# Attention and ReGLU on one core: one written list for the first three tiles, and all lists drawn up anew

## The chip, the cores and the metric

The kernel runs on one core of a Trainium2 chip. Its time is device microseconds (us) of one execution, as the median of several runs. Besides the runs there is one execution that the hardware profiler took; a profile shows that one.

## The reference

```python
# q, k, v: (8 batches, 8 heads, 576, 64); block 64; scale 1/8
scores = scale * q @ k^T, masked to (row // 64 >= column // 64)
attn   = exp(scores - max) / (sum + 1e-09) @ v
x      = attn as (4608 tokens, 512)
out    = (max(x @ w_gate, 0) * (x @ w_val)) @ w_out    # d_ff 1536
```

Blockwise causal attention gives the rows of x, and a gated feed-forward network (ReGLU) follows.

## The kernel before

The feed-forward part is cut into nine tiles of 512 tokens. Tile j, from 0 to 7, is the first 512 tokens of batch j; tile 8 is the eight tails of 64 tokens. Attention runs in visits, one for two heads of one batch: visit r = 4 * batch + pair of heads. A visit computes scores (`s` or `A`, L611), exponentials on ScalarE (`e` or `E`, L616 and L623), zeroes in the corners that the mask excludes (`c` or `C`, L1526 on VectorE, L1529 on POOL), the products with v (`a`, `b` or `V`, L759), a normalisation on VectorE, and a transpose of the result into xT, from visit 4 on by a DMA of SP's queue (`x` or `T`, L842). Attention for a batch is done while the feed-forward part of an earlier tile runs.

Everything is under a manual schedule: each engine executes its instructions in the order in which the program issues them, and waits on semaphores where data or buffers are not ready. So the written order is the order on every queue, SP's and POOL's DMA queues among them.

Tiles 0 to 2 come from a generator, `ffn_gen` (L1156). `ffn(n)` advances it by n matmuls of 512 columns, and the other work of this time, the "acts" (loads, casts, visits of batches 0 to 3, sums of weights), has place numbers in a dictionary `AT`, so that an act is issued when the generator has done that many matmuls. A negative number orders what stands ahead of the first of them. The acts that the text names:

- `j0` to `j4` are filler matmuls on zeros (L1517) that keep TensorE running at the start; `M0` is the first transposing of q and k on TensorE (L420), `p00` the first scores (L561), `x0` to `x3` are the transposes of batch 0's visits into xT.
- `s8` to `s11`, `a8` to `a11`, `b8` to `b11` and `x8` to `x11` are the visits of batch 2: scores, the products with v of the two heads, and the transpose. `s12` opens the visits of batch 3 and is the first to read the transposed tail qTt.
- `d3` and `d4` transpose q and k of batches 3 and 4 (`dma_transposes`: qTm and kTm at L499, qTt at L504, kTt at L506), all on SP's queue; `l4` and `lv4` load batch 4 on POOL's DMA queue (L489).
- `U..` is one sum of weight blocks, `up_sum` (L950); `W..` and `D..` are further weight sums and differences (L901, L904, L915). `on(name)` (L918) gives an operation to POOL if its name is in `ON_POOL`, else to VectorE.

From tile 3 on, a product of matrices is done by seven products of half-size blocks in place of eight, so that sums of blocks on VectorE and POOL replace matmuls. `program(j)` (L1307) returns `do(t)`, which carries out one item of a written list: `ORDER_3_6` for tiles 3 to 6, `ORDER_7` and `ORDER_8`. In these lists `pnw` is work on pair n of hidden blocks: a digit w is half of one of the products (256 columns, L1348), and a letter an operation on the results: `a`, `b` copies on ScalarE (L1371, L1374), `s` a sum (L1377), `m`, `y`, `z` additions out of PSUM on VectorE (L1382, L1393, L1396), `r`, `l` on ScalarE, `H` and `L` the two halves of the hidden product (L1401, and L1415 on VectorE). `s` with four digits forms block sums of the hidden values for the down-projection (L992), `M1` to `M7` are its seven products (L1033), `oa` to `od` and the other `o` items combine them (L1080), and `S` stores. `X` are sums of x (L1154), `g`, `v`, `r`, `h` the pairs that are done with plain products (L1322, L1445).

Buffers rotate by strings too: `SLOTS` gives for each tag (the PSUM banks sc and ffnp, the SBUF tiles ob and gate_sb) which buffer the next tile takes, and `PAIR_BANK` and `AV_BANK` say in which banks the results of a pair or of a visit's products with v lie. A list and these strings are drawn up together.

The corners of a visit in tiles 3 to 6 are issued here:

```python
corners(
    4 * up + i,
    zero_pool if f"{i}C" in ON_POOL else zero_dve,
    (((0, 512),), ((896, 128),))[c],
)
```

`ON_POOL` has no entry that ends in C, so all these memsets run on VectorE.

Of the kernel before, what the change touches and what calls it, by code (L numbers as in the profile page):

```python
# [17 lines left out]
def kernel(  # L18
# [12 lines left out]
    B, H, S, D = q.shape  # L31
# [14 lines left out]
            "010101010101010010101010101010101010101010101010101010101001110010100110"  # L46
            "100111001010011010011100101001101001110010100110100110100101"
        ),
        "ffnp": (
            "021021021020210210210210210210120210120202010101210120201201120120210211"  # L50
            "201021102101020120120120121201202101202101202101210210201102220201101202"
            "001201202112000202112102022102102011022202011012020012012021120002021121"
            "0202210210122001201200121012012"
        ),
        "ob": (
            "043210432104310420312142324014203124304232410421302431423240142031243042"
            "324104210324103140231403"
        ),
        "gate_sb": (
            "021021021021021021021021021021021021021021011201201002102101120120100210"  # L60
            "21021021"
        ),
    }
    ORDER_3_6 = """
        A0 E0t X1 X3 X4 X6 Y4 g0 X7 E0u E0s C01 E0f g0 K g0*2 r0 k g1*2 v0*2 C00 l0 l1
        l2 v0 p15 v0 h0 p15 p1a g1*2 V00 U02 N00 r1 P V01 N01 p12*2 p1b p1s p13 l3 w0
        p13 p1r p11 v1*2 p11 l4 l5 p1m p14 p16*2 p1y d0 p14 p1l v1 U01 U06 U42 l6 l7 l8
        d1 d2 A1 E1u v1 h1 p17*2 p32 E1t E1s E1f p25*2 p32 g8 p1z p1L C11 p22*2 g8*2
        p35*2 C10 s0101 p1H s0112 p2a p23*2 p2b p24 p21 g8 p21 p24 p3b p2r p26 s0012 l9
        l10 d3 w1 p3a p3s s0001 p26 p2s p2m p2y p2H p33*2 p31*2 p3m p2l p27*2 p2z p3r  # L70
        p36*2 p3y r8 p34*2 p3l V11 N11 A2 E2t E2u E2f p2L p37*2 p3z U41 w2 w3 p52*2
        s1101 p55*2 s0212 p3L p5b v8*2 V10 N10 p51 v8*2 h8 p5a p53*2 p51 p54 p5s p5m E2s
        C21 g9*2 p54 s1201 p5r p56 g9 p56 g9 p5l p57 r9 p57 v9*4 p5y p5z C20 h9 M3*2 A3
        E3t p5L s2001 E3s p3H U45 s1012 s2101 s1112 s1001 E3u p5H s2112 U05 E3f U07
        s2012 V21 N21 C31 M4 M3*2 M4 M3*2 U46 U47 w4 w5 C30 V20 N20 M1*3 M4*3 T1 T0 oa
        M5 M1*2 M4 ob V31 M5 V30 M5 N31 M5*2 T2 N30 T3 M1 M5 M2*4 oy M2*2 S0 oz s0201
        s2212 s1212 S1 s2201 M6*2 om M7 M6*3 oc od M7 M6 M7*4 o6 S2 o7
    """
    ORDER_7 = """
        p15 p05 X1 p05 p0a p02*2 p0b p12*2 p1b p01 X3 X4 p03 p0s p03 p0r p15 p1a p04*2  # L80
        p0l p01 p1s X6 p06*2 p13*2 p1r p25*2 X7 p07*2 p0m p0y p0H Y1 p0z p0L p11 p22*2
        p11 P p2a p2b p2s p23*2 p2r p16 p14*2 p1l p16 p1m p1y p24 p26 p21*2 p26 s0101
        p24 p2l p1H p35*2 p3a p2m p2y p32*2 p27*2 p45 p3b p3s p45 p4a s0001 p2H p2z
        p17*2 p1z p33 p34 p33 p55 p42*2 p3r p34 p31*2 p2L p4b p4s p1L p3l p36*2 p55 p5a
        p3m p3y p3H s1101 p43*2 p4r p44 p37*2 p3z p3L s0112 p52 p41 p46 p52 p5b p41 p4m
        p53*2 p5r p5s p51 p44 p4l p51 p46 p4y p54 p47 p56 p54 p4H p5m p56 p5y p5l M4 p47
        p4z p57*2 p5z M3 M4 M3 M1 p5H M4*4 p4L p5L s1012 s1112 M3 s2112 s2101 M3*3 oa
        s0012 s1001 M1*5 M5 s2001 M5 s2012 M5*4 oy S0 ob M2*5 s0212 s0201 M6 s1201 s2212
        M2 M7 s1212 M6 s2201 oz S1 M6 M7 M6*3 om oc od o6 Y3 M7*4 o7 S2
    """  # L90
    ORDER_8 = """
        X6 p12*2 p1b p15*2 p1a p1s X7 p02*2 p0b p05*2 p14 p11*2 p13*2 p0a p0s p1m p01
        p03 p14 p01 p0m p03 p1r p16*2 p1y p1H p1l p17*2 p1z p0r p06*2 p04*2 P p0y p22*2
        p1L p0l p0H p2b s0112 p25*2 p32*2 p35 p07 p35 p2a p2s p07 p0z p0L p23*2 p3a p24
        p21*2 p2m p24 p2r p26*2 p3b p3s p2y p2H p55 p2l p33*2 p31 p34 p31 p34 p3r p36
        s0001 p3m p36 p3y p3H p55 p27*2 s0101 p2z p3l p37*2 p3z p52*2 p51 p5a p42 p45*2
        p5b p54 p53*2 p2L p3L p5s p42 s1001 p41 p4a p43 p41 p51 p43 p5r p56 p5m p56 p54
        p5y p4b p4s p44*2 p4m p5H p4r M3 p46*2 p5l p57 p4l p47*2 p57 M3 p4y p4z p5z M4*2
        p4H M4*3 p4L p5L M1 M4 M3*3 s1012 s1101 s2101 M3 s1112 M1 s2112 M1*3 oa s0012 M5
        s2001 M5 s2012 M5*4 ob oy S0 s2212 M2*5 M1 s0212 s2201 M2 oz S1 s1212 s0201  # L100
        s1201 M6*6 om oc o6 M7*6 S2 od o7b Sb o7a Sa
# [39 lines left out]
        (7, 0): ('one', 'sc', 'sc'),  # L141
# [4 lines left out]
        (7, 5): ('sc', 'ffn', 'ffn'),  # L146
        (8, 0): ('sc', 'ffn', 'ffn'),
        (8, 1): ('ffn', 'one', 'sc'),
        (8, 2): ('sc', 'ffn', 'one'),
        (8, 3): ('ffn', 'sc', 'one'),  # L150
        (8, 4): ('one', 'ffn', 'sc'),
        (8, 5): ('ffn', 'sc', 'ffn'),
# [17 lines left out]
    AV_BANK = {0: ('sc', 'one'), 1: ('ffn', 'ffn'), 2: ('sc', 'ffn'), 3: ('ffn', 'sc')}  # L170
    U_AT = {'U15': 300, 'U12': 306, 'U11': 312, 'U16': 386, 'U17': 389, 'U25': 320, 'U22': 326, 'U21': 332, 'U26': 392, 'U27': 395, 'U35': 340, 'U32': 346, 'U31': 352, 'U36': 398, 'U37': 401, 'U55': 360, 'U52': 366, 'U51': 372, 'U56': 404, 'U57': 407}
# [1135 lines left out]
    def program(j):  # L1307
# [128 lines left out]
        def do(t):  # L1436
# [38 lines left out]
            elif k == "C":  # L1475
# [3 lines left out]
                    zero_pool if f"{i}C" in ON_POOL else zero_dve,  # L1479
# [51 lines left out]
    with tc.manual_schedule(engines={E.PE, E.DVE, E.Activation, E.Pool, E.SP}):  # L1531
# [82 lines left out]
        def mains_1(hp):  # L1614
# [8 lines left out]
        AT = {  # L1623
            "p00": -41,
            "p02": -40.5,
            "cq4": -40,
            "cq6": -39.5,
            "M1q": -39,
            "M1k": -38.5,
            "p01": -38,  # L1630
            "c0": -37.5,
            "j3": -37,
            "p11": -36.5,
            "M2q": -36,
            "p10": -35.5,
            "M2k": -35,
            "p12": -34.5,
            "j2": -34,
            "M3q": -33.5,
            "M3k": -33,  # L1640
            "cv0": -32.5,
            "cv2": -32,
            "c1": -31.5,
            "p20": -31,
            "a0": -30.5,
            "p21": -30,
            "b0": -29.5,
            "p22": -29,
            "a1": -28.5,
            "b1": -28,  # L1650
            "p31": -27.5,
            "x0": -27,
            "cv00/01": -26.5,
            "cv00/23": -26,
            "cg00/01": -25.5,
            "p30": -25,
            "cv4a": -24.5,
            "cv4b": -24,
            "cg00/23": -23.5,
            "x1": -23,  # L1660
            "p32": -22.5,
            "c2": -22,
            "c3a": -21.5,
            "c3b": -21,
            "cv6a": -20.5,
            "a2": 3,
            "b2": 3.01,
            "cv6b": 3.02,
            "C1": 3.03,
            "a3": 6,  # L1670
            "b3": 6.01,
            "x2": 6.02,
            "x3": 8,
            "g01": -53.5,
            "v01": -53.4,
            "g10": -49.5,
            "v10": -49.4,
            "g11": -49.3,
            "v11": -49.2,
            "g20": -0.39,  # L1680
            "v20": -0.38,
            "g21": 7.2,
            "v21": 8.18,
            "cg01/01": 4.1,
            "cg01/23": 10,
            "cv01": 8.2,
            "cg10": 8.21,
            "cv10": 8.27,
            "cg11": 8.28,
            "cv11": 8.29,  # L1690
            "cg20": 30.89,
            "cv20": 31,
            "cg21": 31.91,
            "cv21/0": 32.24,
            "ev0a": 32.33,
            "ev0b": 32.34,
            "Lq0": -63.5,
            "Lq2": -62.27,
            "Lv0": -61.59,
            "Lv2": -59.5,  # L1700
            "Lq6": -59.5,
            "Lq4": -59.5,
            "v00": -58.48,
            "g00": -56.5,
            "Lv4": -54.8,
            "Lv6": -54.8,
            "C0": -47.5,
            "j0": -46.5,
            "cq0": -45.5,
            "cq2": -44.33,  # L1710
            "M0": -41.18,
            "j1": -41.2,
            "j4": -41.17,
            "E1q0": 20.29,
            "w01": 32.1,
            "w00": 32.11,
            "w11": 32.11,
            "w20": 32.12,
            "w10": 32.12,
            "E1v0": 32.16,  # L1720
            "w21": 32.16,
            "E1q6": 32.19,
            "E1q4": 32.19,
# [351 lines left out]
```

## Time and profile before

| | us |
| --- | --- |
| median of 3 runs (lowest, highest) | 348.47 (348.32, 348.5) |
| profiled execution, own time | 348.39 |
| span of the profiled execution, first to last instruction | 346.6 |
| granted TensorE clock, mean | 0.999 of full speed |
| busy: PE 334.8, PE weight loads (PEld) 233.9, VectorE (DVE) 273.0, ScalarE (ACT) 207.5, POOL 194.7 | of 346.6 |
| tile periods: start of 3, 4, 5, 6 | 140.1, 176.2, 212.4, 248.3 |

The profile gives busy time, waits and a chain of waits from one execution. A wait is put down to the engine whose signal came last. Matmuls are pipelined and their ends are modelled, so that the pace of TensorE is read from start to start. About one per cent of the matmul records is missing, so that a single doubled distance can be a missing record.

### The profile page before, as it was taken

What the parts mean: (1) busy time and instruction counts of PE and PEld (TensorE: products, weight loads), DVE (VectorE), ACT (ScalarE), POOL (GpSimd) and SP (SyncE); (2) the same over time, 40 slices, a digit from 0 to 9 for tenths busy, and PEclk for the clock granted to TensorE, in tenths of its full rate; (3) what the DMA queues carried; (4) which work ended last, traced back from release to release, by engine and by line L of the source; (5) the groups of instructions that cost most, each with busy time, mean ns of one, the idle gap of its engine ahead of it and who ended that gap; (6) DMA issues with size and microseconds to landing.
All of it is one profiled execution on the core that took longest, in us unless ns stands there. A gap on an engine that the chain in (4) does not pass through costs nothing.

```text
span 346.6 us, 9051 instructions
## 1 busy us (share of the span) xinstructions
PE 334.8 (97%) x3481; PEld 233.9 (67%) x3518; DVE 273.0 (79%) x690; ACT 207.5 (60%) x341; POOL 194.7 (56%) x229
## 2 busy tenths in 40 slices
PE   8999999999999999999999999999999999999994
PEld 4544455545545559676977787778778788888873
DVE  4854455768629897789977997899899989999995
ACT  4942756587335872687468746884588537526721
POOL 2767566477795901986087627872155636612530
PEclk9999999999999999999999999999999999999999
DMA  8999999999999994999299929993400141012005
GB/s 244 294 352 373 360 217 242 229 155 176 184 218 113 137 191 82 190 174 139 40 158 181 152 40 156 164 171 47 121 32 2 33 129 33 2 41 83 3 0 121
DMA packets 155403, 50.07 MB, mean 144 GB/s; under 512 B 134464, under 2 KB 151744, under 8 KB 155360
## 3 DMA queue, kind: packets, MB, share of 16 engines
q1 hardware_dynamic: 77520, 32.52, 43.7%
q0 software_dynamic: 70528, 8.98, 43.3%
q10 hardware_dynamic: 7312, 8.00, 8.3%
q8 instruction: 27, 0.44, 0.5%
q14 instruction: 16, 0.13, 0.1%
HBM read 37.75 MB, written 9.44 MB: 136 GB/s over the span
## 4 chain that ended last, share of the span: by engine, by line
PE 75%; DMA 10%; DVE 9%; issue 2%; ACT 2%; POOL 1%; DVEq 0%; SPq 0%; ACTq 0%; POOLq 0%
PE ffnp L1033 11%; PE ffnp L1162 11%; PE ffnp L1348 9%; PE ffnp L1322 7%; PE sc L1348 7%; PE ffnp L1265 5%; PE one L1348 5%; PE one L1033 4%; PE sc L611 3%; DMA stage<-in_moe_w_out_dram 3%; PE ffnp L759 3%; DMA stage<-in_moe_w_val_dram 2%; DMA stage<-in_moe_w_gate_dram 2%; PE one L611 2%; DVE ob L1382 2%
## 5 line engine op out<-in xcount | busy, mean ns | idle before, releaser
L616 ACT ACTIVATE attnT<-sc 128x1024 bf16<-128x1024 f32 x56 | 56.3, 1037 | 0.0
L1033 PEld LDWEIGHTS <-stage 128*128 128x128 bf16 x420 | 39.9, 98 | 4.8 <-DVE stage L992 0.2
L992 DVE TENSOR_TENSOR stage<-hT 128x512 bf16<-128x512 bf16 (+2 forms) x120 | 39.6, 382 | 0.2
L1162 PE MATMUL ffnp<-xT,wg 128*128 128x512 bf16 x130 | 36.2, 379 | 0.6
L1172 ACT ACTIVATE gate_sb<-ffnp 128x512 bf16<-128x512 f32 x35 | 20.5, 598 | 27.0 <-PE ffnp L1162 22.7
L1080 POOL TENSOR_TENSOR ob<-ob,ob 128x512 f32<-128x512 f32 x7 | 8.9, 1268 | 45.7 <-DVE ob L1080 19.9
L1348 PEld LDWEIGHTS <-stage 128*128 128x128 bf16 x288 | 27.6, 98 | 7.4 <-issue 0.4
L759 PEld LDWEIGHTS <-attnT 128*128 128x128 bf16 x640 | 26.1, 98 | 9.2 <-DVE attnT L1526 1.1
L1033 PE MATMUL ffnp<-stage 128*128 128x256 bf16 x252 | 32.0, 273 | 0.0
L1162 PE MATMUL ffnp<-xT,wv 128*128 128x512 bf16 x108 | 31.3, 380 | 0.2
L1182 DVE TENSOR_TENSOR hT<-gate_sb,ffnp 128x512 bf16<-128x512 bf16 x28 | 19.1, 684 | 14.1 <-PE ffnp L1162 11.5
L623 ACT ACTIVATE attnT<-one 128x512 bf16<-128x512 f32 (+1 forms) x28 | 15.0, 536 | 22.2 <-PE ffnp L611 11.6
L489 POOL DMA_DIRECT2D v_bf<-in_v_dram x30 | 24.5, 826 | 3.5 <-PE sc L759 1.6
L1348 PEld LDWEIGHTS <-wg 128*128 128x128 bf16 x224 | 21.5, 98 | 5.7 <-issue 1.5
L1348 PEld LDWEIGHTS <-wv 128*128 128x128 bf16 x224 | 21.8, 98 | 4.1 <-DVE perm L1154 0.2
L1265 PE MATMUL ffnp<-wo,hT 128*128 128x512 bf16 x91 | 23.2, 379 | 0.3
L1162 PEld LDWEIGHTS <-wv 128*128 128x128 bf16 x144 | 12.9, 98 | 14.7 <-issue 1.8
L1162 PEld LDWEIGHTS <-wg 128*128 128x128 bf16 x144 | 13.4, 98 | 13.8 <-issue 0.5
L1401 POOL TENSOR_TENSOR hT<-gate_sb,ob 128x512 bf16<-128x512 bf16 x16 | 19.0, 1188 | 4.0 <-DVE ob L1393 3.9
L489 POOL DMA_DIRECT2D q_bf<-in_q_dram x20 | 18.0, 906 | 3.7 <-DVE recip L732 3.5
L611 PEld LDWEIGHTS <-kTm 64*128 64x128 bf16 x384 | 11.3, 94 | 12.9 <-issue 7.3
L1377 POOL TENSOR_TENSOR ob<-ob,ob 128x512 f32<-128x512 f32 x8 | 10.1, 1265 | 16.7 <-ACT ob L1371 10.2
(228 smaller groups left out, 911.7 us busy)
## 6 DMA issues: line engine op xcount, KB each, us to landing
out_dram<-ob ACTq DMA_DIRECT2D x28, 256.0 KB, 3.6
stage<-in_moe_w_val_dram SPq DMA_DIRECT2D x6, 512.0 KB, 8.7
stage<-in_moe_w_gate_dram SPq DMA_DIRECT2D x6, 512.0 KB, 8.3
stage<-in_moe_w_out_dram SPq DMA_DIRECT2D x6, 512.0 KB, 10.5
q_bf<-in_q_dram POOLq DMA_DIRECT2D x20, 128.0 KB, 4.8
k_bf<-in_k_dram POOLq DMA_DIRECT2D x20, 128.0 KB, 5.9
v_bf<-in_v_dram POOLq DMA_DIRECT2D x20, 128.0 KB, 6.3
stage<-in_v_dram SPq DMA_DIRECT2D x19, 128.0 KB, 5.4
```

Source lines behind the costliest of these rows:

```text
L489: ins = nc.gpsimd.dma_start(dst, part_of)
L611: nc.tensor.matmul(o, kTm[b % 2][head_of(hh), c, hp, :], qT, start=True, stop=True)
L616: return lambda: nc.scalar.activation(at[:, :, lo : lo + 512], sc, AF.Exp, scale=scale)
L759: nc.tensor.matmul(av[:, p, :], at[:, col : col + 128], v_bf[b % 2][:, c, h, :], start=(p == 0), stop=(c == p), skip_group_check=True,)
L992: nc.vector.tensor_tensor(out=out.rearrange("p (c n) -> p c n", c=m), in0=a, in1=b, op=op)
L1033: nc.tensor.matmul(to, sums.of(c)[which][:, 128 * p : 128 * p + 128], right, start=first, stop=(c == 5), skip_group_check=True,)
L1162: nc.tensor.matmul(to, (wg, wv)[t][f // 4][:, c, 128 * (f % 4) : 128 * (f % 4) + 128], x[:, c], start=(c == 0), stop=(c == 3),)
L1172: nc.scalar.activation(gate_sb, gate, AF.Relu)
L1182: nc.vector.tensor_tensor(out=h, in0=gate_sb, in1=val, op=AX.mult)
L1265: nc.tensor.matmul(op, hT[f][:, 128 * s : 128 * (s + 1)], wo[f // 4][:, f % 4, n0:n1], start=(f == 0), stop=(f == 11),)
L1322: nc.tensor.matmul(to, (wg, wv)[t][f // 4][:, c, 128 * (f % 4) : 128 * (f % 4) + 128], x[:, c], start=(c == 0), stop=(c == 3),)
L1348: nc.tensor.matmul(st[key][:, 256 * k : 256 * k + 256], left[:, c, 128 * k : 128 * k + 128], right[:, c], start=new and (k, c) == (0, 0), ...
```

## The change

Tiles 0 to 2 get a written list, `ORDER_0_2`, in place of `AT`, `U_AT` and the numbers for W and D: an item is an act, and `f*n` advances the feed-forward generator by n matmuls. All the other lists, with `SLOTS`, `PAIR_BANK`, `AV_BANK` and `ON_POOL`, are replaced by new ones, and the corner memsets of tiles 3 to 6 are looked up by tile, visit and corner, so that those named in `ON_POOL` run on POOL.

```diff
+    ORDER_0_2 = """
+        j0 Lq0 C0 Lq2 cq2 Lq4 cq4 cq0 j1 j4 j3 M0 p00 M1q Lv0 cv0 Lq6 cq6 Lv2 cv2 v00
...
+        a1 g10 cg10 C1 p31 x1 p30 v10 cv10 c2 a2 p32 c3b c3a b2 f*4 a3 g11 cg11 g20 v11
+        cv6b cg20 cv11 b3 x2 f*4 x3 cg01/23 f*6 g21 v20 cg21 cv20 f*14 v21 cv21/0 E1q0
...
+        f*3 A1 f a8 f*5 u2k o1 c9 f B1 f*2 s10 e10 f*5 b8 f*3 a9 f*4 b9 f*14 u3 s11 f*6
+        l3 f*5 c10 b10 e11 c11 a10 f S2 f E2 f*2 lv3 f*3 b11 f*3 a11 W1 W2 W3 f*9 D0 f
+        L2 f*7 x9 x8 W4 W5 U12 f*6 D5 D3 f x10 f*6 x11 f*11 U21 U55 D1 U52 f*2 l4 A2
+        f*15 d3 s12 B2 lv4 f*9 e12 f*4 D2 U22 c12 s13 U15 f*5 D4 f*2 L3 f*2 b12 f o2 e13
+        o3 a12 x12 f*2 c13 U17 U35 U26 f*8 s14 f*3 a13 b13 x13 U32 f*5 e14 c14 f*7 s15
+        f*4 d4 a14 f b14 x14 f*10 U16 U25 e15 c15 f*6 b15 U31 f U27 U57 U11 a15 f x15
+        f*5 U56 U51 U36 U37 f*24
+    """.split()
     ON_POOL = set(
         """
-        2oc 2od 31H 32H 33H 33s 35H 35s 3od 41H 42H 43H 43s 45H 45s 4od 51H 52H
-        53H 53s 55H 55s 5od 61H 62H 63H 63s 65H 65s 6od 70H 71H 71s 72s 73H 73s
-        74H 74s 75H 75s 7od 81H 82H 82s 83H 83s 84H 84s 85H U02 U06 U07 U41 U42
-        U45 U46 U47
+        2oc 2od 32H 33H 33s 35H 35s 3C01 3C10 3C11 3C21 3C30 3C31 42H 43H 43s
+        45H 45s 4C01 4C10 4C11 4C21 4C30 4C31 52H 53H 53s 55H 55s 5C01 5C10 5C11
+        5C21 5C30 5C31 62H 63H 63s 65H 65s 6C01 6C10 6C11 6C21 6C30 6C31 70H 71H
+        71s 72s 73H 73s 74H 74s 75H 75s 7od 80s 81H 82H 82s 83H 83s 84H 84s 85H
+        8od U01 U02 U06 U07 U11 U12 U15 U16 U17 U26 U27 U32 U42 U46 U47 U52 U55
+        U56
         """.split()
     )
-    AV_BANK = {0: ('sc', 'one'), 1: ('ffn', 'ffn'), 2: ('sc', 'ffn'), 3: ('ffn', 'sc')}
+    AV_BANK = {0: ('one', 'sc'), 1: ('ffn', 'ffn'), 2: ('ffn', 'ffn'), 3: ('sc', 'sc')}
...
-                    zero_pool if f"{i}C" in ON_POOL else zero_dve,
+                    zero_pool if f"{j}C{of}" in ON_POOL else zero_dve,
...
-        AT = {
...
-            "j3": -37,
...
-            "M0": -41.18,
-            "j1": -41.2,
-            "j4": -41.17,
...
-            "a11": 259.02,
-            "b11": 259.11,
-            "x11": 259.97,
-            "d3": 260.7,
...
-            "l4": 319.56,
...
-            "s12": 326,
...
-        for n in sorted(acts, key=lambda n: AT[n]):
-            at = int(AT[n])
-            ffn(at - place[0])
-            place[0] = max(place[0], at)
-            acts[n]()
+        for item in ORDER_0_2:
+            t, _, times = item.partition("*")
+            if t == "f":
+                ffn(int(times or 1))
+            else:
+                acts[t]()
         ffn(10**6)
```

Of the 24 corner memsets on POOL, six stand in each of the tiles 3 to 6. In those tiles p1H and od move to VectorE; in tile 8, p0's sum (80s) and od (8od) move to POOL. Eleven weight sums of tiles 0 to 2 move to POOL, and U41 and U45 of tile 6 change places with U01. TensorE has the same 3518 matmuls as before, of the same sizes; VectorE has 584 instructions in place of 591 and POOL 214 in place of 177, with those that only wait counted. `ORDER_3_6`, `ORDER_7` and `ORDER_8` hold the same items as before, in another order.

More of the change, by code (lines that the diff above doesn't have):

```diff
@@ L96 @@
[L96 to L101, printed above, removed]
+        p12*2 p1b p15*2 p1a X6 X7 p02*2 p0b p05*2 p14 p13*2 p0a p0s p1r p11*2 p1s p1m
@@ L140 @@
         (6, 5): ('ffn', 'one', 'sc'),
-        (7, 0): ('one', 'sc', 'sc'),
+        (7, 0): ('sc', 'sc', 'ffn'),
         (7, 1): ('ffn', 'ffn', 'one'),
```

339 lines of the change are left out of this document (58 added, 281 removed).

## The prediction

> **What bounds the kernel now.** I read the page first, then busy time by stage, then the idle time ahead of single instructions.
>
> ```profile
> PE 334.8 (97%) x3481; PEld 233.9 (67%) x3518; DVE 273.0 (79%) x690; ACT 207.5 (60%) x341; POOL 194.7 (56%) x229
> ...
> PE   8999999999999999999999999999999999999994
> ```
>
> TensorE (PE) is busy from the first slice to the last, but a busy share hides small stalls. From start to start, a matmul of 512 columns takes 0.216 us in this trace, one of 256 columns 0.109, one of 65 columns 0.031. The program's matmuls add up to about 320 us of such pitch. The excess over them is the most that any list can win: 7.4 us in the first 20, 5 after PE's last matmul (341.7 to 346.6), and about 15 in between, of which I find some 5 in places where PE waits for a named engine. The rest is 0.1 us here and there at changes of row group, which stay. By stage (columns: window, sum, PE, PEld, DVE, ACT, POOL, clock, DMA share, GB/s):
>
> ```profile
> 100.00:140.10 40.10, 39.83 (x427) 24.57 (x431) 32.64 (x95) 21.34 (x34) 20.86 (x27) 1.00 1.34 148
> 212.40:248.30 35.90, 35.54 (x413) 27.60 (x416) 31.34 (x83) 24.14 (x41) 21.46 (x24) 1.00 1.30 132
> 284.30:313.50 29.20, 28.66 (x256) 24.42 (x254) 27.89 (x56) 14.95 (x29) 13.98 (x11) 1.00 0.12 40
> 313.50:346.60 33.10, 27.37 (x243) 23.03 (x240) 27.75 (x56) 14.49 (x27) 10.55 (x9) 0.99 0.18 46
> ```
>
> Tiles 3 to 6 (second row) are PE's, with 4.5 us of VectorE (DVE) to spare; tiles 7 and 8 (last two rows) have both engines full: 29.0 and 29.25 us a tile against 27.28 of matmul pitch. The largest single stall lies in tile 8, and the chain of waits shows DVE just before it:
>
> ```profile
> 331.84 1.29 DVE ob L1396 x2
> 333.12 0.66 DVE hT L1415 x2
> 333.78 0.46 issue
> ```
>
> In the timeline (start, length, what; in brackets the idle time before it and who ended it) PE waits there, and from start to start 0.81 us are lost:
>
> ```profile
> 333.00 0.83 PE L1033 MATMUL one<-wo,hT 128*128 128x256 bf16 x6 [0.65 <-POOL hT L1401]
> ```
>
> In tiles 3 to 6 the one that recurs is the second bank of A1's scores, behind a DVE addition:
>
> ```profile
> 147.97 0.39 PE L611 MATMUL sc<-qTm,kTm 64*128 64x384 bf16 x4 [0.28 <-DVE ob L1393]
> ```
>
> **The change, part by part.** PE gets the same matmuls, ACT the same operations. DVE loses 7 instructions net, POOL gains 37 with its waits; SP issues the same DMAs, reordered.
>
> *Tiles 3 to 6.* Six corner memsets a tile go from DVE to POOL (24 in all):
>
> ```profile
> L1526 DVE MEMSET attnT<- x62: 165/165/165, 9.1 to 276.5; 64x128 uint32 x62
> L1529 POOL MEMSET attnT<- x2: 307/307/307, 129.2 to 129.5; 64x256 bf16 x2
> ```
>
> That is 6 x 0.165 = 0.99 us off DVE. Two operations come back to it, p1H (0.68) and od (0.69): DVE +0.38 a tile. POOL: 6 x 0.307 - 1.19 (p1H) - 1.27 (od) = -0.6. With 4.5 us idle, DVE's 0.38 costs nothing by itself; p1H leaves POOL's 1.19 us for DVE's 0.68 on the path to the next sums. What counts is the order around A1: its banks are freed further ahead. I find 0.3 to 0.5 us of stalls a tile and take 0.1 of it away from three tiles: -0.3. Upper end +1.2 (each tile's POOL corner late by its own 0.3), lower end -1.0.
>
> *Tile 7.* DVE has the same 56 operations, but directly chained pairs (the second reads what the first wrote) fall from 10 to 8. A 128x512 f32 operation follows an independent one after 0.60 us, a chained one after 0.80, seen at 331.01 and 331.84 against 331.84 and 332.44. 2 x 0.19 = 0.38, most of it on the path since DVE is full: -0.3 (-0.9 to +0.5, by the stalls of 1.3 us there).
>
> *Tile 8.* 80s and 8od go to POOL: two operations of 0.60 us less on DVE, and one chained pair more, 0.19: -1.0 of DVE's 28 us. 80s stood in front of p5L, the hidden product that ends in PE's gap of 0.81 us at 332 to 333. I put 0.7 on the path, with -1.2 (nearly all stalls of the tile) and +0.2 as ends. 8od itself takes 1.27 us instead of 0.69, beside o6's products: 0 (+-0.3).
>
> *Startup.* The filler products j1, j4, j3 now all stand before M0, three more matmuls of 512: M0 moves from 4.91 to 5.56, +0.65, and the first exp of ACT from 6.51 to 7.16. But before, the exp chain had pauses of 0.29 and 0.25 us, and PE stood 0.37, 0.33 and 0.2 us between 17 and 19.8. Walking the new order with these durations, x3's transposes, which all of tile 0 waits for, come at 19.4 instead of 19.5: -0.1 (+-0.5).
>
> *Tiles 0 to 2.* Eleven sums of weights (U) go to POOL: 11 x 1.17 = 12.9 us there, 11 x 0.41 = 4.6 off DVE, between 100 and 140, where DVE has 7.5 us idle and POOL 19. The first products that read them come with tile 3, and 6 us of POOL stay free: 0, and if the last one is late, up to its own 1.2 us. The list also moves batch 2's last attention products (a11). Before they stand at feed-forward matmul 259, with s12, which opens batch 3's visits, at 326; now at 269 and 327. Counting all PE work, a11 comes 2.2 to 2.8 us later, s12 0.14 later. Behind a11 hangs x11, the transpose, and behind that on SP's queue the four of batch 3 (d3):
>
> ```profile
> 91.98 4.51 SPq L842 DMA_TRANSPOSE xT<-xnat  x2
> 96.66 3.87 SPq L499 DMA_TRANSPOSE qTm<-q_bf  x1
> 100.76 3.33 SPq L499 DMA_TRANSPOSE kTm<-k_bf  x1
> 104.20 1.18 SPq L504 DMA_TRANSPOSE qTt<-q_bt  x1
> 105.49 2.12 SPq L506 DMA_TRANSPOSE kTt<-k_bt  x1
> 109.67 0.19 PE L611 MATMUL one<-qTt,kTm 64*128 64x64 bf16 x1
> ```
>
> qTt was issued at 104.20 and landed 4.0 us later, at 108.2; s12 read it at 109.67: 1.45 us of slack. By the delay of a11, less up to 0.2 for the pauses of the queue, it is now issued at 106.2 to 107.0, and lands at 109.6 (with the trace's shortest 3.4) to 113.3 (longest 6.3); s12 wants it at 109.81. At 4.0 to 4.4 (this one, and the median) the wait is 0.4 to 1.6 us. Behind s12 in PE's queue wait feed-forward products that need nothing from it, so the wait is lost in full. I take +0.6, near the landing this transfer had, ends -0.1 and +3.4.
>
> **Sum.** -0.1 + 0.6 - 0.3 - 0.3 - 0.7 = -0.8, from the profiled execution's 348.39 us (span 346.6 and 1.8 around it; the median of the runs is 348.47): 347.6.
>
> **A rule against the change.** DVE and POOL do hinder each other here. Operations of DVE with two inputs in SBUF stretch when a POOL operation is under way:
>
> ```profile
> 255.23 1.15 POOL L950 TENSOR_TENSOR attnT<-wv 128x512 bf16<-128x512 bf16 x1
> 255.84 0.82 DVE L950 TENSOR_TENSOR attnT<-wg,wv 128x512 bf16<-128x512 bf16 x1
> ```
>
> Alone, this sum takes 0.41 us; it ends 0.29 after POOL's end at 256.38. Likewise L1415 took 0.92 instead of 0.68 at 289.12. But an L992, which also reads two, took 0.426 against 0.411 where it began 0.13 us before POOL's end, and of 184 such operations only 12 began inside one of POOL at all: the price is up to 0.6 us for each meeting, and meetings are rare. The Trainium skill ("SBUF — State Buffer", section "SBUF: two separate sides") states an exclusive lock on a shared port pair, held for the whole instruction, that a DVE operation with two SBUF inputs contends for only against a GpSimd operation that reads SBUF; by it the 24 memsets, which read nothing, would be free and the sums would not. The trace agrees on the sums; no row shows a memset that meets such an operation. By the page, then, only the eleven sums and 80s would cost what rival 3 gives; by the rows alone the memsets too may stretch a DVE operation, each by at most its own 0.307, beside PE work with 4 us of DVE to spare a tile.
>
> **Rivals.**
> 1. *The transposes of d3 come late (slower).* For it: slack of 1.45 us against 2.2 to 2.8 us of delay, and POOL's loads (l4) in the DMA queues from 106.5, earlier than the 107.6 before. Against: landings vary between 3.4 and 6.3 us, and the short ones leave nothing to wait for. Landing at about 6 us, the wait is 2.4 to 3.4: 348.39 - 1.4 + 3.4 = 350.4. It decides from a wait of 2.1 us on, where the change is slower than before by over 0.2%. Chance 0.26.
> 2. *DVE's relief is absorbed (same).* For it: PE and DVE are both full in tiles 7 and 8, so a stall removed makes the other engine the next to wait, and the turns of all buffers are redrawn. Against: PE's pitch leaves 3.7 us in the two. Then -0.1 + 0.6 - 0.3 - 0.2 = 0: 348.4. Chance 0.22.
> 3. *Meetings of the new POOL operations with two-input ones of DVE (slower).* For it: the four rows with 0.24 to 0.41 us of stretch. Against: how seldom the two met. Eleven sums and 80s meet one each at 0.33 (mean of the four stretched rows): 4 us of DVE, of which 1 reaches PE in tiles 0 to 2 (as much as all its named stalls from 20 to 140 now), and tile 8's gain is gone: 348.39 - 0.1 + 0.6 + 1.0 - 0.3 - 0.3 = 349.3. Chance 0.09.
> 4. *s12 finds its transpose landed, and tiles 7 and 8 lose most of their 2.8 us of named stalls (faster).* For it: four of the stalls stand behind DVE, which gets 1 us back; against: DVE stays full. 348.39 - 0.1 - 0.5 - 1.0 - 1.1 = 345.7. Chance 0.1.
>
> That the corner rule takes no effect is excluded: the built program has those memsets on POOL.
>
> **The numbers.** The forecast itself, 347.6, has 0.33. A measurement of this kernel tells 0.2%, 0.7 us, from no change. Faster: most of the forecast's 0.33 and rival 4, 0.42. Same: rival 2 and a tail of the forecast, 0.23. Slower: rivals 1 and 3, 0.35. The range 346.0 to 350.4 leaves out the far side of rivals 4 and 1. The forecast's own range is 346.4 to 348.2.
>
> **What would show it.** Right: qTt lands 0.3 to 1.5 us after PE is at s12, the only new stall over 0.5 us; the gap before L1033 near 333 shrinks from 0.81 to under 0.4; tile 7 takes 28.7 us; x3's transposes lie at 19.4. Wrong: s12 waits over 2 us, or not at all; tile periods of 3 to 5 leave 35.9 to 36.2 by over 0.3; PE's stalls in 7 and 8 sum to 2.8 us as before; DVE rows on L950 or L992 stretch in 100 to 140.

## The result, and the profile after

The changed kernel takes 354.37 us (median of four runs, 354.2 to 354.79) against 348.39 for the kernel before on the same chip (348.24 to 348.5): a ratio of 1.0174, 95% interval 1.0156 to 1.0191. It is 6.0 us slower, where 347.6 was forecast and 350.4 was the top of the range. The profiled execution took 354.26 us, with a span of 352.5. One run further down, of 358.08 us, was in a slower state of the chip and is left out of its kernel's ratio.

First the line of busy times on the page after (engine, busy us, share of the span, instructions):

```profile
PE 337.8 (96%) x3518; PEld 234.2 (66%) x3518; DVE 278.4 (79%) x662; ACT 208.4 (59%) x341; POOL 207.6 (59%) x257
```

DVE has 28 instructions fewer than before and is busy 5.4 us longer. By the prediction's prices, and counting two sums that changed places (U41 and U45 on DVE now, U01 not), it should have lost about 4: 4.6 less for the eleven sums, 1.4 less for tile 8's two operations, 1.5 more for p1H and od less the 24 memsets, 0.4 more for the two sums against the one. Some 9 us of DVE time have appeared inside instructions that were there before. The busy times by stage, after (window, length, then busy time of PE, PEld, DVE, ACT, POOL, clock, DMA share, GB/s), at the same places as before:

```profile
104.10:144.20 40.10, 38.50 (x420) 23.82 (x419) 33.22 (x84) 20.99 (x33) 28.57 (x32) 1.00 1.36 146
216.70:252.60 35.90, 35.76 (x417) 27.41 (x416) 31.46 (x79) 24.19 (x41) 20.59 (x27) 1.00 1.43 125
289.70:319.00 29.30, 28.76 (x257) 24.66 (x255) 27.79 (x56) 14.92 (x29) 13.67 (x11) 1.00 0.12 39
319.00:352.50 33.50, 27.18 (x243) 23.06 (x240) 26.79 (x54) 14.39 (x27) 13.24 (x11) 0.98 0.19 47
```

The left edges give the ledger. Tile 3 starts at 144.2 instead of 140.1: 4.1 us are lost before it. Tile 5 starts 4.3 us late, tile 7 5.4, tile 8 5.5, and the span ends 5.9 us late. Tiles 3 to 6 add 1.3, tiles 7 and 8 add 0.5 to the end of the span, 0.3 of it by PE's last matmul. In the first 144 us the lag, read at places with equal matmul work behind them, goes in four steps: 1.3 us at 23 (and 1.0 to 1.3 up to 54), 2.4 at 62, 2.8 at 109.5, 4.1 at 131.6. The rows of PE's timeline after where this happens, with two that the prediction had named (start, length, what; in brackets the idle time before and who ended it):

```profile
6.28 0.39 PE L443 MATMUL ffnp<-ident,q_bf 128*128 128x128 bf16 x4
59.93 0.48 PE L782 MATMUL one<-v_bf,attnT 128*128 128x65 bf16 x10 [0.99 <-DVE attnT L1549]
112.79 0.19 PE L634 MATMUL one<-qTt,kTm 64*128 64x64 bf16 x1
126.46 0.46 PE L782 MATMUL ffnp<-v_bf,attnT 128*128 128x65 bf16 x10 [1.20 <-DVE hT L1205]
152.16 0.40 PE L634 MATMUL sc<-qTm,kTm 64*128 64x384 bf16 x4 [0.27 <-DVE ob L1416]
255.58 0.29 PE L663 MATMUL one<-qTt,kTt 128*128 128x64 bf16 x4 [0.94 <-DMA kTt<-k_bt]
338.20 0.38 PE L1056 MATMUL ffnp<-stage 128*128 128x256 bf16 x2 [1.19 <-DVE ob L1419]
```

**Start.** M0, the first row, stands at 6.28 instead of 4.91, 1.37 later. **Visit 7** waits 0.99 for a corner memset of DVE at 59.93. **s12**, at 112.79, waits for nothing. **Batch 3** waits at 126.46 behind a gate product of DVE. **A1's stall** at 152.16 is as it was (0.28 before). **Tiles 4 and 6** wait for kTt, a transpose (0.28 and 1.11 us lost from start to start; the second is the row at 255.58). **Tile 8's stall** is still there, at another product, 338.20, and is longer: 1.35 us from start to start against 0.81.

What was going on on DVE and POOL around the steps at 59.9, 106 and 126 (timeline after, a few rows of each engine):

```profile
57.95 1.00 DVE L369 CAST k_bt<-stage 64x256 bf16<-64x256 f32 x1
100.94 5.06 DVE L938 TENSOR_TENSOR wo<-wo 128x256 bf16<-128x256 bf16 x2
101.34 1.14 POOL L927 TENSOR_TENSOR stage<-wo 128x512 bf16<-128x512 bf16 x1
104.66 1.19 POOL L973 TENSOR_TENSOR stage<-wv 128x512 bf16<-128x512 bf16 x1
105.92 0.68 DVE L1298 COPY ob<-ffnp 128x512 f32<-128x512 f32 x1
122.98 1.25 DVE L973 TENSOR_TENSOR stage<-wg 128x512 bf16<-128x512 bf16 x1
124.15 1.66 DVE L1015 TENSOR_TENSOR stage<-hT 128x1024 bf16<-128x1024 bf16 x1
```

Two weight differences (L938), each 0.28 alone, take 3.9 and 1.2 us while POOL works without a pause: at the end of a long row of sums for W (the last of them L927 at 101.34) and then at three of the moved sums (L973), the last from 104.66 to 105.85. As soon as POOL is through, the copy at 105.92 runs, which PE has been waiting for: 0.37 us are lost at 106.07, and 0.36 more at 108.95, there behind ACT by the row. A sum that stayed on DVE (L973) takes 1.25 instead of 0.41 at 122.98, where POOL is at the end of its DMA issues; the next addition takes 1.66 instead of 0.69, beside a moved sum on POOL from 123.95 to 125.26; and the gate product behind them (L1205) ends late for PE. Even a cast (1.00 instead of 0.29, beside POOL's own casts) is stretched at 57.95, and the corner memset behind it is late.

The queue of SP, after, for the two transposes in question:

```profile
106.81 1.18 SPq L527 DMA_TRANSPOSE qTt<-q_bt  x1
250.09 1.20 SPq L768 DMA_TRANSPOSE xTt<-xtail  x1
251.39 2.26 SPq L529 DMA_TRANSPOSE kTt<-k_bt  x1
```

The qTt of batch 3 was issued at 106.81, inside the 106.2 to 107.0 of the prediction, and landed 4.5 us later, at 111.3; PE, itself 2.9 us late by then, reached s12 only at 112.67. The kTt of tile 6 is issued at 251.39, at the end of tile 5 and behind four transposes of x; before, it was issued at 230.16. PE wants it at 254.47 and loses 1.11 us there.

### The profile page after: what moved, and what is told of

The parts are those of the page before. It is cut to its first block, busy times and chain, and to the rows that moved or that the text cites. A ratio compares the mean times of both kernels' runs of the same rounds, so it can differ in the third digit from the quotient of the medians.

```text
span 352.5 us, 9071 instructions
## 1 busy us (share of the span) xinstructions
PE 337.8 (96%) x3518; PEld 234.2 (66%) x3518; DVE 278.4 (79%) x662; ACT 208.4 (59%) x341; POOL 207.6 (59%) x257
## 4 chain that ended last, share of the span: by engine, by line
PE 77%; DVE 8%; DMA 5%; issue 4%; SPq 2%; ACT 1%; POOL 1%; DVEq 0%; ACTq 0%; POOLq 0%
PE ffnp L1185 14%; PE ffnp L1371 10%; PE ffnp L1056 9%; PE sc L1371 8%; PE ffnp L1345 6%; PE ffnp L1288 6%; PE one L1371 4%; PE one L1056 4%; PE sc L634 3%; DMA kTt<-k_bt 2%; PE ffnp L782 2%; PE one L1185 2%; PE one L634 2%; PE sc L782 2%; DMA stage<-in_moe_w_gate_dram 2%
## 5 line engine op out<-in xcount | busy, mean ns | idle before, releaser
L1015 DVE TENSOR_TENSOR stage<-hT 128x512 bf16<-128x512 bf16 (+2 forms) x120 | 42.5, 402 | 0.1
L1185 PE MATMUL ffnp<-xT,wg 128*128 128x512 bf16 x140 | 37.5, 379 | 0.4 <-DVE ob L1298 0.2
L1056 PE MATMUL ffnp<-stage 128*128 128x256 bf16 x252 | 32.8, 273 | 1.7 <-DVE ob L1419 1.7
L1185 PE MATMUL ffnp<-xT,wv 128*128 128x512 bf16 x112 | 31.9, 380 | 0.0
L1205 DVE TENSOR_TENSOR hT<-gate_sb,ffnp 128x512 bf16<-128x512 bf16 x28 | 19.2, 684 | 14.7 <-PE ffnp L1185 11.0
L1552 POOL MEMSET attnT<- 64x256 bf16 x26 | 7.9, 328 | 38.3 <-ACT attnT L646 24.3
L1185 PEld LDWEIGHTS <-wg 128*128 128x128 bf16 x144 | 13.4, 97 | 14.6 <-issue 1.8
L1185 PEld LDWEIGHTS <-wv 128*128 128x128 bf16 x144 | 13.2, 98 | 14.3 <-issue 1.1
L646 ACT ACTIVATE attnT<-ffnp 128x512 bf16<-128x512 f32 (+1 forms) x28 | 15.1, 538 | 9.4 <-PE ffnp L634 9.3
L1345 PE MATMUL ffnp<-xT,wg 128*128 128x512 bf16 x64 | 20.5, 380 | 0.0
```

The source lines that it names most:

```text
L646: nc.scalar.activation(at[:, hh, 1024 : 1024 + w], third[hh][:, 0:w], AF.Exp, scale=scale)
L1015: nc.vector.tensor_tensor(out=out.rearrange("p (c n) -> p c n", c=m), in0=a, in1=b, op=op)
L1056: nc.tensor.matmul(to, sums.of(c)[which][:, 128 * p : 128 * p + 128], right, start=first, stop=(c == 5), skip_group_check=True,)
L1185: nc.tensor.matmul(to, (wg, wv)[t][f // 4][:, c, 128 * (f % 4) : 128 * (f % 4) + 128], x[:, c], start=(c == 0), stop=(c == 3),)
L1345: nc.tensor.matmul(to, (wg, wv)[t][f // 4][:, c, 128 * (f % 4) : 128 * (f % 4) + 128], x[:, c], start=(c == 0), stop=(c == 3),)
```

## The experiments

Ratios are against the kernel before on the same chip, and "lag" means how late PE is, in the profiled execution, against the trace of before with equal matmul work behind it.

**One suspect at a time.** The first filler products go back behind M0:

```diff
-        j0 ... cq0 j1 j4 j3 M0 p00 M1q ... M1k cv4a
+        j0 ... cq0 j1 M0 j4 p00 M1q ... M1k j3 cv4a
```

> Changed kernel with the filler products put back: j4 and j3 again behind M0 (j1 M0 j4 p00 ... M1k j3), nothing else. Theory: the three extra fillers ahead of M0 run at the slow pace of the start (0.425 us each, not 0.216), so M0 comes 1.37 us late and tile 0 starts 1.3 us late; this gives 353.1 (1.0 to 1.5 less than 354.4). Rival, by my prediction's walk: the start is bound by the chain of exponentials and by loads, fillers cost nothing in the end; then 354.2 to 354.5.

Measured: 355.22 (353.8 to 356.19), ratio 1.019 [1.0161, 1.0218]. A miss: the lag at 10 us is 0.9 less than in after, but from 19 us on nothing of that is left (1.45 at 23, against 1.33), and PE comes to 109.5 as late as without the edit. Five profiled executions with the filler places of after (after, e2, e3, e4, e8) are 0.7 to 1.8 late at 23, so one execution here can't show what the fillers are worth. In the profiled execution of this kernel (356.19, its slowest) three waits for kTt cost about 3.4 us.

The last DVE casts of a load go behind visit 7's exp and corners:

```diff
-        ... b6 td0 e7 c7
+        ... b6 e7 c7 td0
```

> Changed kernel with the casts of batch 0's tails (td0) moved behind the corner memsets of visit 7 (e7 c7 td0 for td0 e7 c7). Theory: VectorE's two casts, stretched from 0.29 to 1.0 and 0.64 us beside POOL's operations, stand ahead of the memsets that TensorE's products wait for at 58.7; without them in front the wait of 1.15 us there is gone and the time is 353.2 (353.1 to 353.5). Rival: the wait moves to the next product of the tile, the time stays within 0.3 of 354.4.

Measured: 354.52 (354.29 to 355.64), ratio 1.0179 [1.0161, 1.0197]. The wait at 59 is gone, and the time is the same. In the profiled execution of the kernel above, where nothing was edited there, it was gone too: it comes and goes. The kernels with the eleven sums on POOL and the lists of after start the same product of PE (L1185, x by the gate weights) at 109.34 (after), 109.42 (e1), 109.42 (e2) and 109.52 (e4), whatever their lag was at 62 (2.4, 1.4, 1.9 and 1.5): the gain at visit 7 is lost later, at the sums. The pair of L938 is held in all four; in this kernel:

```profile
100.52 5.56 DVE L938 TENSOR_TENSOR wo<-wo 128x256 bf16<-128x256 bf16 x2
```

Its second operation alone takes 5.2 us here, to 106.07, where the last of POOL's row has ended at 105.92. In e1 it is 5.2 as well, and in e4 the first of the pair takes 5.9.

The eleven sums go back to DVE:

```diff
     ON_POOL:
-        8od U01 U02 U06 U07 U11 U12 U15 U16 U17 U26 U27 U32 U42 U46 U47 U52 U55 U56
+        8od U01 U02 U06 U07 U42 U46 U47
```

> Changed kernel with the eleven sums of weights of tiles 0 to 2 back on VectorE; the lists stay. Theory: VectorE's two-input operations are held up by POOL's back-to-back sums (one took 3.9 us instead of 0.28 at 100.9); with the sums on VectorE, 4.6 us more work for it, those rows shrink to under 1.7, the waits of TensorE at 106, 109 and 125 (2.1 us together) go, and the time is 352.4 (352.0 to 353.2). Rival: it is the order of the list, or VectorE's load, that makes them wait; then VectorE is later still and the time is 354.4 to 356.

Measured: 351.59 (350.46 to 353.27), ratio 1.0093 [1.0062, 1.0124]: 2.8 us of the 6.0 come back. The time is better than the expected range. The product of 109.34 starts at 107.77, and tile 3 starts with a lag of 2.0 instead of 4.1; of this lead 0.6 is there at 23 us already, before any of the sums. Against e1, which is as late at 100 us (1.1 and 1.2), it is ahead by 2.5 at 128. The pair of weight differences that took 5.06 us, in this kernel's timeline:

```profile
100.09 1.06 DVE L936 TENSOR_TENSOR wo<-wo 128x256 bf16<-128x256 bf16 x2
```

DVE does the eleven sums itself here (4.5 us) and is busy 274.5 us against 278.4: the eleven on POOL stretched DVE by 8.4 us in all. PE then waited longer for kTt and lost 1.3 us of the gain there.

The loads l9, l10 and the transpose d3 go to an earlier place in tiles 3 to 6:

```diff
-  ... h8 l7 l8 p5b ... p5m d1 d2 T1 r9 ... s1212 l9 p5H ... M5*2 l10 d3 oz ...
+  ... h8 l7 l8 l9 l10 p5b ... p5m T1 d1 d2 d3 r9 ... s1212 p5H ... M5*2 oz ...
```

> Changed kernel with one edit in the list of tiles 3 to 6: loads l9 and l10 follow l8, and d3 (the transpose of the k tails) follows d2, with T1 ahead of d1. Theory: kTt, issued last on SP's queue after T2 and T3, is late for the next tile by 0.28, 0 and 1.1 us (waits at 182 and 254); with it ahead of T2 these waits go: 353.0 (352.9 to 353.4). Rival: T2 and T3 are pushed back on the queue by the transpose's 1.2 to 2.2 us and xT comes late for the next tile instead: 354.4 to 356.

Measured: 351.81 (351.44 to 353.03), ratio 1.0092 [1.0075, 1.0108]: 2.6 us come back. SP's queue in this kernel, the transpose for tile 6:

```profile
245.64 1.96 SPq L529 DMA_TRANSPOSE kTt<-k_bt  x1
```

It is issued 5.7 us earlier, PE waits nowhere for it, and the lag is 4.2 to 4.5 us from tile 3 to the end, so that the new lists of tiles 3 to 6 lose next to nothing but that. This profiled execution was the slowest of its kernel (353.03), 1.2 below that of the changed kernel, of which kTt is 1.4. Where the rest of the 2.6 lies, in runs without a trace, is not shown.

All four edits together:

> Changed kernel with the four edits of e1 to e4 together. After those runs my theory is that POOL's unbroken row of additions, from 93.7 to 105.9, sets a gate at 106: whatever is won ahead of it (fillers, corner memsets) is lost there, since VectorE's weight differences wait for its end. With the sums off POOL the gate is gone, and the other edits count: 348.6 (348.0 to 349.6). Rival: the edits overlap, e1 and e2 stay without effect, and only e3 and e4 count: 351.59 - 2.5 = 349 to 350.5 with PE at the same distance behind before at 23 us and at 62 us as in e3.

Measured: 350.16 (349.4 to 351.33), ratio 1.0056 [1.0036, 1.0076]. 4.2 us come back, about the sum of the single ones (2.8 + 2.6 - 0.85 - 0.15 = 4.4). That is above the range of the theory (348.0 to 349.6) and inside that of the rival. The lag is 1.7 to 2.4 us from 23 to 135, and 2.3 to 2.9 from then on.

**The new lists of tiles 3 to 8 alone.** The kernel before, with the new lists, banks and corner rule of tiles 3 to 8, and its own tiles 0 to 2:

```diff
     (before)
-    SLOTS, PAIR_BANK, AV_BANK, ORDER_3_6, ORDER_7, ORDER_8, ON_POOL of before
+    the same of after, without its eleven U; AT and U_AT kept as before
```

> Kernel of before for tiles 0 to 2 (its places, the sums on VectorE), and the new lists, buffers and POOL assignments for tiles 3 to 8, corner memsets on POOL included. Theory: what the change loses in tiles 3 to 8 is the late kTt, 1.4 to 2.5 us, and the rest of the new lists is worth about nothing: 349.9 to 351. Rival: the lists for 3 to 8 are better as I forecast (-1.3) and kTt, with tiles 0 to 2 unhurried, is in time: 347.1 to 347.6.

Measured: 349.88 (349.61 to 350.24), ratio 1.0044 [1.0028, 1.0061]. PE waits for kTt here too (0.62 us lost from 178.96 on). The same with the earlier l9, l10 and d3:

> h1_lists with the list edit of e4_d3 (kTt transposed ahead of T2). h1 lost 0.6 us to kTt in its profile and 0.3 to 0.4 more at A1 in tile 3. Theory: with kTt in time the new lists for tiles 3 to 8 are worth nothing: 348.3 to 349.0. Rival: they hold the gain that I forecast, -1.3: 347.0 to 347.4.

Measured: 348.5 (ten runs, 348.33 to 349.7), ratio 1.0001 [0.9985, 1.0017]. The edit returns 1.4 us here. With kTt in time, the new lists of tiles 3 to 8 are worth nothing, either way. In tile 8 PE still waits 0.84 us behind DVE, at 333.72: the relief of DVE was absorbed there.

**The lock by itself.** Operations that no one needs are put on POOL in the kernel before, where DVE makes its sums:

```diff
+        def busy_pool():
+            for _ in range(3):
+                nc.gpsimd.tensor_tensor(out=zeros, in0=zeros, in1=zeros, op=AX.add)
+        acts["Z"] = busy_pool
+        AT["Z"] = 305.5
```

> Kernel of before with three additions of 128x512 bf16 on POOL that nobody reads, placed ahead of the weight differences of tiles 0 to 2, where POOL is idle (from 104.0 to 107.4). Theory: a two-input operation of VectorE that begins meanwhile is held until the last of the three ends, 1.5 to 2 us long instead of 0.28, although each of the three lasts only 1.15; TensorE waits 0.5 to 1.5 us for the hidden products behind it. Rival: the two share, or VectorE gets its turn between two operations of POOL: no row over 1.3 us.

With `memset(zeros, 0.0)` seven times instead:

> As l1_pool_adds, but with seven memsets of 128x512 bf16 (0.53 us each, 3.7 us in all) in place of the three additions. Theory, by the row of memsets of tiles 3 to 6 beside L1015: POOL operations that read nothing hold up no operation of VectorE; its rows keep 0.28 and 0.41 us. Rival: any POOL operation holds the other engine up; then they stretch as in l1_pool_adds.

Measured: 348.25 and 348.65 (one execution each). These two test nothing: both were over before DVE's sums began (the additions at 104.9, the sums at 105.35). So again with five additions, then with ten memsets:

> As l1_pool_adds, where the three additions began at 101.7 and were over when VectorE's weight differences began, with five of them, so that POOL is busy until 107.2. Theory: the first two-input operation of VectorE after 105 (L915, 0.28 us alone) lasts until the last of them ends, over 1.5 us although one addition lasts 1.15, and TensorE waits 0.5 to 1.5 us for the hidden product behind it. Rival: VectorE gets in between two additions: no row over 1.3 us.

Measured: 349.94 (one execution). POOL and DVE in this kernel's timeline:

```profile
101.71 5.83 POOL L2032 TENSOR_TENSOR zeros<-zeros 128x512 bf16<-128x512 bf16 x5
105.39 1.25 DVE L915 TENSOR_TENSOR wo<-wo 128x256 bf16<-128x256 bf16 x2
106.56 1.25 DVE L950 TENSOR_TENSOR stage<-wv 128x512 bf16<-128x512 bf16 x1
```

A pair that takes 0.48 beside nothing takes 1.25, a sum of 0.41 takes 1.25, and PE is 1.6 us late from 106 on. Each is held to the end of one addition, and gets in before the next. These additions start 0.08 us after the end of the one before (at 104.13 behind 104.06, for one), since each reads what that one wrote.

> As l3_pool_adds, where the weight differences and sums of VectorE from 105.4 on each waited for the end of an addition of POOL (1.25 us in place of 0.48 and 0.41), with ten memsets of 128x512 bf16 in place of the five additions (about 5.6 us). Theory: they read nothing and hold up nothing; VectorE's rows from 105 on keep 0.48 and 0.41 and the time that of before, unless POOL ends later than 107.5. Rival: any POOL operation holds VectorE up; rows of 0.7 us and more.

Measured: 348.27 (one execution). The same place with ten memsets:

```profile
103.46 5.76 POOL L2032 MEMSET zeros<- 128x512 bf16 x10
105.39 0.48 DVE L915 TENSOR_TENSOR wo<-wo 128x256 bf16<-128x256 bf16 x2
105.80 0.42 DVE L950 TENSOR_TENSOR stage<-wv 128x512 bf16<-128x512 bf16 x1
```

Nothing is stretched. The Trainium skill ("SBUF — State Buffer", section "Who interferes with whom") has an exclusive lock on the port pair that DVE and GpSimd share. These two runs agree with it on what takes the lock: additions, which read, hold DVE off, and memsets do not.

**One part of the change on the kernel before.** The 24 corner memsets of tiles 3 to 6 on POOL, with the old lists:

```diff
     ON_POOL:
+        3C01 3C10 3C11 3C21 3C30 3C31 4C01 ... 6C31
-                    zero_pool if f"{i}C" in ON_POOL else zero_dve,
+                    zero_pool if f"{j}C{of}" in ON_POOL else zero_dve,
```

> Kernel of before with the one part: the 24 corner memsets of tiles 3 to 6 on POOL (the new key and its entries), all lists as before. Theory: VectorE has 4.5 us to spare in these tiles, and memsets hold up no operation of VectorE, so the time is the same within 0.3 us: 348.1 to 348.7. Rival: POOL's 0.3 us each, queued behind 1.2 us additions, make the products with v late in four tiles: 349 to 351.

Measured: 366.06 (364.77 to 367.24), ratio 1.0505 [1.0477, 1.0534]. Both theories missed by far. Tile 3 in this kernel's timeline:

```profile
141.73 0.31 POOL L1530 MEMSET attnT<- 64x256 bf16 x1 [1.74 <-ACT attnT L617]
150.79 0.67 POOL L1530 MEMSET attnT<- 64x256 bf16 x2
151.54 1.16 POOL L1402 TENSOR_TENSOR hT<-gate_sb,ob 128x512 bf16<-128x512 bf16 x1
152.73 0.96 DVE L993 TENSOR_TENSOR stage<-hT 128x256 bf16<-128x256 bf16 x3 [1.55 <-POOL hT L1402]
156.21 0.60 PE L1349 MATMUL ffnp<-perm,stage 128*128 128x256 bf16 x4 [2.06 <-DVE ob L1383]
```

POOL works in order. A memset must wait for ACT's exp (25.1 us of POOL's idle time in this kernel end that way), and what stands behind it is late: here POOL's DMA issues from 142.25 on and the hidden product L1402, at 151.54 instead of 148.66. DVE waits 1.55 for that product and then takes 1.75 for a sum of 0.69 beside POOL's DMA issues, and PE waits 2.06 for DVE. The new lists place the same memsets so that this costs nothing (the ratio of 1.0001 above); they also take p1H and od off POOL. The old ones do not, at 18 us, of which an estimated 3.4 are TensorE at half clock: behind two stands of PE, of 3.12 and 2.57 us, the granted clock is 0.50 for 3.4 us each.

The eleven sums on POOL, with the old lists:

```diff
     ON_POOL:
+        U11 U12 U15 U16 U17 U26 U27 U32 U52 U55 U56
```

> Kernel of before with the one part: the eleven sums of tiles 0 to 2 on POOL, places as before. They stand there between POOL's DMA issues of batch 4, not in a row. Theory: VectorE's two-input operations meet them one at a time, each meeting costs up to 1 us on VectorE, which has 7.5 us to spare; also l4's and lv4's loads are pushed back by up to 5 us: 348.6 to 350. Rival: taken off VectorE they only help, 348.0 to 348.5.

Measured: 353.31 (351.55 to 358.08), ratio 1.0129 [1.008, 1.0178]. The sums alone make the kernel before slower, by 4.5 us by the ratio and by 3.4 by the median of the three runs without that of 358.08 (351.7). Both expectations missed. In its timeline DVE meets four sums in a row on POOL, from 120.53 to 125.1:

```profile
122.61 2.82 DVE L993 TENSOR_TENSOR stage<-hT 128x512 bf16<-128x512 bf16 x1
```

PE then stands 2.07 us, up to 126.17, and goes from 0.6 us ahead to 1.5 late. Behind this stand TensorE's clock halves:

```profile
126.17 0.61 PE L1163 MATMUL ffnp<-xT,wv 128*128 128x512 bf16 x2 [1.90 <-DVE xtail L706]
128.00:129.00 1.00, 1.00 (x3) 0.30 (x2) 0.03 (x1) 1.00 (x2) 0.00 (x0) 0.50 1.30 221
```

From 127.1 to 130.5 the granted clock is 0.50, a product of 512 columns takes 0.427 instead of 0.216, and PE is 3.1 us late from 131.6 on: the meeting cost 2.1 directly, and 1.6 more through the clock.

Three of the eleven back to DVE in the changed kernel, those that POOL made during the long pair at 100.94:

```diff
-        8od U01 U02 U06 U07 U11 U12 U15 U16 U17 U26 U27 U32 U42 U46 U47 U52 U55
+        8od U01 U02 U06 U07 U11 U15 U16 U17 U26 U27 U32 U42 U46 U47
         U56
```

> Changed kernel with three of the eleven sums back on VectorE: U12, U52 and U55, which stand right behind the ten sums W on POOL. Theory: these three make POOL's unbroken row last from 100.8 to 105.85, and that row, through VectorE's weight differences, sets the gate at 106; without them TensorE passes there 1.2 to 1.6 us earlier, while the wait at 125, beside other sums, stays: 352.9 to 353.5 less what kTt takes back (up to 1). Rival: the number of sums counts, not where they stand: 3 of 11, so 353.6 or more with the gate still at 109.5.

Measured: 353.38 (350.66 to 354.59), ratio 1.0137 [1.0092, 1.0182]. At 106 nothing is lost any more (lag 2.2 at 100, 2.3 at 115), and the stall of batch 3 stays, 1.49 us at 124.62. In the profiled execution, the slowest of the four, kTt took the gain back, with 1.2 and 1.0 us.

**The start.** The all-edits kernel, with its list up to x3 drawn after the sequence of before:

```diff
-        j0 Lq0 C0 Lq2 cq2 Lq4 cq4 cq0 j1 M0 j4 p00 M1q Lv0 cv0 Lq6 ... x3
+        Lq0 Lq2 Lv0 Lv2 Lq6 Lq4 v00 g00 ... C0 j0 cq0 cq2 j1 M0 j4 p00 p02 ... x3
```

> e5_all with the start of the list, up to x3 and the first 8 products, in the order of before (and before's buffers for it). After e5_all my theory is that what is left of the loss, 2 us, lies ahead of 20 us: in the new start the exponentials wait longer, whatever the fillers cost. Then tile 0 begins as in before and the time is 348.3 to 348.9. Rival: the start is won back or lost again at the weights and loads behind it, and the lists of tiles 0 to 2 and 3 to 8 hold the rest: 349.6 to 350.2.

Measured: 352.93 (352.46 to 353.73), ratio 1.0127 [1.0101, 1.0153]. The edit also moved two loads of v ahead of loads of q and k: POOL's cast of q waited 2.43 us, and the start lost 2.8 to 3.2 us, part of it at half clock (PE stood 2.62 us, and the granted clock is 0.50 from 11.5 to 15.0). With the loads in the sequence of before (`Lq0 Lq2 Lv0 Lq4 Lq6 Lv2`):

> e6_startup had the loads of v ahead of two loads of q and k on SP's queue, which before has not (a cast of q waited 2.4 us for them); this kernel has them in the order of before, all else as e6_startup. Theory, unchanged: what e5_all still loses lies ahead of 20 us, in the new order of the start; with that of before the time is 348.3 to 349.0. Rival: the lists of tiles 0 to 2 and 3 to 8 hold the rest: 349.6 to 350.2.

Measured: 349.78 (349.19 to 350.28), ratio 1.0049 [1.0032, 1.0066]. The lag at 23 us is 0.4 instead of 1.7, but the median gains only 0.4 on the all-edits kernel, which is within the spread of the two.

## Why the prediction was wrong

**The eleven sums: +2.8 where the forecast had 0 and rival 3 had 1.** This is the main step that failed. The mechanism was named, with its rows, and the Trainium skill's rule beside it; the price and the chance of 0.09 were off. "Up to 0.6 us for each meeting, and meetings are rare" came from four rows of later tiles, which stretch DVE by 0.24 to 0.41, each behind one POOL operation; the longest such row of the trace of before, a sum at 101.34 that takes 1.04 instead of 0.41 in the very tiles where the sums go, was left out of the price. The change placed three sums behind a row of POOL that was long already, where DVE makes differences of weights. There the price of one meeting was 3.6 us (3.9 instead of 0.28) in the changed kernel and 4.9 to 5.6 in three of its variants (5.2, 5.2 and 5.9), and with four sums in a row in the kernel before it was 2.4 (2.82 instead of 0.41): the held operation did not get in between two sums. The eleven sums stretched DVE by 8.4 us, where rival 3 had 4. Putting them back returned 2.8, and adding them to the kernel before cost 3.4 to 4.5, in its profiled execution 1.6 of it through the half clock that a long stand of PE was followed by. The five useless additions let DVE in at the end of each. What decides between the two was not found. Those additions stand 0.08 us apart, while in a row of sums the next starts about 0.03 before the one ahead ends; but DVE got in without such a pause too, at 104.7 in the changed kernel and at 102.1 in the kernel before.

**kTt: +2.6, not priced at all.** The prediction followed d3 in tiles 0 to 2 and only there. In tiles 3 to 6 it priced "the order around A1" and not SP's queue, on which the transpose had moved behind those of x. Moving it forward returned 2.6. In the profiled execution of the changed kernel it cost 1.4, in those of its variants with the late d3 1.3 to 3.4, and with the old tiles 0 to 2, where the same edit returned 1.4, 0.6.

**d3 in tiles 0 to 2: +0.6 was forecast, 0 seen.** Issue and landing were as worked out; that PE itself would come 2.9 us late, by the other steps, took the wait away. Rival 1, at 0.26, was not what happened.

**Start: -0.1 forecast, +1.3 in the trace.** Three fillers were priced at 0.216 each. In the trace after, TensorE was still at half pace there, and each filler of 512 columns took 0.427. The first filler runs at 1.0 us, and the change of pace came between 3.7 us (h2) and 6.9 us (e8) of the span, different for each execution (before 4.8, after 6.2), while the granted clock in the profile's rows says 1.00 throughout (the trace's first record of the clock stands at the change, so nothing was recorded ahead of it). The Trainium skill ("TensorE: Matmul & The Clock Gate", section "What you observe") puts the change around 4 us into sustained activity, with half a microsecond of variation: these traces show the same factor of two, but 2.7 to 5.9 us after the first filler, a wider variation. But moving the fillers gave no time back, and redrawing the whole start some 0.4, so how much of the 1.3 reaches the end is not shown.

**Tiles 7 and 8: -1.0 forecast, nothing.** Rival 2 was right here. DVE got its two operations back in tile 8, and PE still waits, at another product. The prediction's own sign of being wrong came true: the stalls of the two tiles add up to 2.9 us before and 2.9 after. In the changed kernel PE's last matmul even adds 0.3; with kTt in time on the old tiles 0 to 2, all of tiles 3 to 8 differ by 0.15 us from before, within the measurement. The pair read as chained at 331.01 is none (the first writes k_bf, the second reads and writes ob), though true pairs show the same: 0.81 at 322.05, for one.

**Tiles 3 to 6: -0.3 forecast.** A1's stall stayed at 0.27. The 24 memsets cost no more than forecast, but for a reason that was not given: n1 and h2 show that memsets of the same kind cost 18 us or nothing, by the lists around them. That the new places stand late enough behind the exps is the likely reading; p1H and od, which left POOL, may have a part in it. The relief of DVE had no value, as the prediction said of its 0.38.

**Still open.** With the sums back, kTt early and the start redrawn, 1.5 us are left over the kernel before (349.78 against 348.3). Only the fastest of the four executions has a trace, 0.9 above: there 0.4 are lost before 23 us, 0.1 from 23 to 128, and 0.3 behind that. Where the other 0.6 of the median lie is not shown; the order of tiles 0 to 2 after x3 was not tried by itself. No version here beats the kernel before.

## What to carry to other kernels

Before moving a two-input addition from DVE to POOL, list what DVE will execute in that stretch: where POOL will run several in a row beside DVE's own two-input operations, let the price of a meeting go up to the length of the whole row of POOL operations, not of one. When a list is redrawn, follow each queue that works in order (SP's transposes, POOL's memsets behind an exp) from its issue to the wait of its reader, in every stage and not only in the one that looked tight. And a relief of an engine in a stage where two are full should be priced at nothing until a run shows otherwise.

## What the runs showed of the hardware

- A DVE operation of 0.28 us was held for 3.9 us, over the end of one POOL sum and three more in a row, and in three other traces 5.2, 5.2 and 5.9 us; one of 0.41 was held for 2.82, over the end of one and two more. Five additions in one tile, 0.08 us apart, let DVE in at the end of one (1.25 for 0.41 and for a pair of 0.48). A sum of 0.41 took 1.25 beside POOL's DMA issues, and one of 0.69 took 1.75.
- Ten POOL memsets in a row beside the same DVE operations stretched none of them (0.48 and 0.42).
- A DVE cast from f32 beside POOL's casts took 1.00 instead of 0.29.
- TensorE's pace at the start of an execution doubled at 3.7 us in one execution, at 6.9 in another and between them in the rest, while the rows show a granted clock of 1.00, without a record of the clock ahead of the change.
- Behind stands of PE of 2.07, 2.57, 2.62 and 3.12 us the granted clock was 0.50 for 3.4 us, and a product of 512 columns took 0.427 (n2, n1, e6). Behind two other stands in n1, of 2.22 and 2.71 us, it was not.
